# A dilated gated convolution on one core: the steps of every unit in another order

## The chip, the cores and the metric

The kernel runs on one core of one Trainium2 chip. The metric is device time in microseconds; the median of three runs before the change is 309.94 us (309.79 to 312.44).

## The reference, cut to what matters

```python
B, T, D, K = 2, 16000, 144, 15          # x [B,T,D], w [K,D,2D], w_o [D,D], all bfloat16
xp = jnp.pad(x, ((0, 0), (28, 0), (0, 0)))
h = sum(einsum('btc,cd->btd', xp[:, 28 - 2*i : 28 - 2*i + T, :], w[i]) for i in range(K))
z = jnp.tanh(h[..., :D]) * sigmoid(h[..., D:])
return z @ w_o
```

It is a causal convolution with 15 taps two steps apart, 144 channels in and 288 out, then a gate (tanh of one half times sigmoid of the other) and a 144 by 144 projection.

## The kernel before, in words

Time is cut into ten blocks of 3072 steps and one of 1536. A block is two units (units 0 to 19), the last block is unit 20. The convolution is computed in a fast form with fewer products: sums and differences of shifted inputs (tiles `S`, `D`, `E` and the shorter `S2`, `D2`, `E2`, `S4`, `D4`, `E4`, `E42`, and the same of the last 16 channels, `Sr`, `Dr`, `Er`) are multiplied on TensorE (PE) by sums of the weights, and the results are combined on VectorE (DVE).

In each unit the four products `m` = 0 to 3 start in a pair of PSUM banks (`px`, a pool of two pairs, `x_bank`). `V.m` computes a common part there, `Vk.m` copies it on ScalarE (ACT) to the second bank, `Vp.m` adds the private parts. For `m` = 0 and 1, `C` copies the result to single banks (`py`, a pool of three, `y_bank`), `X` and `Y` add further taps in both places, and `tX`, `tY` take them away as `m0`, `m1`. For `m` = 2 and 3, `v.m` takes the pair away as `v2`, `v3`, and `A`, `Ak`, `Ap` compute a second part in another pair or in two single banks. A pair is free for the next user when the instruction that takes it away has run: `tX` or `v` on ACT, or, for a pair that `A` used, `At` on DVE.

On DVE the joining instructions of a unit are `P` (m0 + m1), `s` (m0 - m1, four columns of `y`), `U` (P + v2), `At.2...` (y from U and the second part of product 2), `u3q` (P minus v3, in place) and `At.3...` (y from P and the second part of product 3). `U` reads what `P` wrote, the first `At.2` what `U` wrote, the first `At.3` what `u3q` wrote. All of them are line 205 in the profile, told apart by their tiles: `P<-m,m`, `y<-m,m`, `U<-P,v`, `y<-U,...`, `P<-P,v`, `y<-P,...`.

DVE also derives the input sums: an even unit makes the `E` tiles of its own block, an odd unit the `S`, `D`, `Sr` and `Dr` tiles of the next block. `gt`, `gs` (ACT) and `gm` (DVE) are the gate, which writes `z`. `zT` is a DMA on SP's queue that transposes `z`; `po.g` projects three twelfths of it on PE, `o.g` (ACT) moves the result to `os`, and `ST` stores it. `LD` stands behind `zT`: in an even unit it issues the two transposing loads of `rx` (the last 16 channels of the next block, for both planes e = 0, 1), in an odd unit the loads of `xn`. `Dr` and `Sr` in the next odd unit read `rx`.

The order in which each engine gets its instructions is written out by hand, in four lists of step names (`FIRST` for unit 0, `ODD`, `EVEN`, and `FINAL` for unit 20); a name ending in `.n` is a step of the next unit. Every instruction passes through `K_`, which keeps program order within its engine. The pools give their banks in the order in which the steps ask for them.

Of the kernel before, what the change touches and what calls it, by code (L numbers as in the profile page):

```python
# [15 lines left out]
def kernel(  # L16
# [26 lines left out]
    P = 128  # L43
    B, T, D = x.shape
    K = w.shape[0]
    D2 = w.shape[2]
# [328 lines left out]
    for j in range(8):  # L375
        o = 16 * j
# [187 lines left out]
    U = [dict(id=i, r=r, bi=bi) for i, (bi, r) in enumerate(units)]  # L564
# [238 lines left out]
    def run(ui, names):  # L803
# [1 line left out]
            step(ui, name)  # L805

    FIRST = """
        B wn0.0 wn0.1 wd.1 wd.0 wh.1 wh.0 S D S2 S4 D2 E D4 E2 Sr Dr E4 Er E42 w.0 wt.0 z.15 V.0 w.1 z.3 z.9 z.1 z.5 V.1 Vk.0 wt.1
        w.2 Vk.1 wt.2 Vp.0 w.3 Vp.1 z.12 C.0.1 wt.3 w.8 C.0.0 Y.0.1.main X.0.0.main wn wt.8 w.9 z.10 z.7 wt.9 C.1.0 Y.0.0.main w.4
        X.0.1.main wt.4 X.1.0.main w.5 Y.0.0.rest Y.1.0.main wt.5 tY.0.0 C.1.1 w.6 X.0.0.rest X.0.1.rest Y.1.0.rest X.1.0.rest X.1.1  # L810
        Y.0.1.rest wt.6 tX.0 V.2 tY.1.0 Y.1.1 tX.1 Vk.2 tY.0.1 A.2.1 Vp.2 A.2.0 tY.1.1 Ak.2.1 v.2 Ak.2.0 P U w.7 Ap.2.1.0 V.3 Vk.3
        wt.7 Ap.2.1.1 Ap.2.0.1 At.2.1 Vp.3 Ap.2.0.0 v.3 V.0.n A.3.1 Vk.0.n X.3.0 X.3.1 s At.2.0.0 At.2.0.1 Ak.3.1 Vp.0.n Ap.3.1.0
        Ap.3.1.1 gt.6 C.0.0.n wx u3 tX.3 At.3.1.0 C.0.1.n gs.6 At.3.1.1
    """
    EVEN = """
        B Y.0.0 V.1 Vk.1 tY.0.0 gt.0 X.0.1 X.0.0 Vp.1 po.1 Y.0.1 C.1.0 tX.0 C.1.1 E Y.1.0 X.1.1 V.2 X.1.0 o.1 tY.1.0 gs.0 tY.0.1 Vk.2
        tX.1 Y.1.1 Er E4 E2 gm.6.p A.2.0 Vp.2 po.2 A.2.1 gm.0 E42 zT LD tY.1.1 P Ak.2.0 v.2 Ak.2.1 U A.3.1 Ap.2.0.0 V.3 Ap.2.1.1
        Ap.2.1.0 At.2.0.0 At.2.1 s Vk.3 o.2 Vp.3 v.3 po.3 Ap.2.0.1 A.3.0 V.0.n At.2.0.1 u3q Ak.3.1 o.3 Vk.0.n Ak.3.0 gt.6 ST LL
        Ap.3.1.1 Ap.3.1.0 Vp.0.n Ap.3.0.0 Ap.3.0.1 po.0 At.3.1.0 At.3.1.1 At.3.0 C.0.0.n C.0.1.n gs.6 o.0
    """  # L820
    ODD = """
        B D Y.0.0 X.0.0 X.0.1 V.1 Y.0.1 gt.0 Vk.1 tX.0 tY.0.0 Vp.1 po.1 C.1.0 C.1.1 V.2 Y.1.0 gs.0 Vk.2 o.1 tY.0.1 S Dr X.1.1 X.1.0
        Y.1.1 Vp.2 tY.1.0 tX.1 tY.1.1 v.2 po.2 A.2.1 A.2.0 Ak.2.1 Ak.2.0 o.2 A.3.1 V.3 Ap.2.1.0 Vk.3 Ap.2.1.1 Ap.2.0.0 Vp.3 Ap.2.0.1
        Sr SD4 gm.0 SD2 gm.6.p zT LD P U At.2.1 At.2.0.0 A.3.0 po.3 v.3 Ak.3.0 Ak.3.1 V.0.n Ap.3.0.1 s At.2.0.1 u3q Vk.0.n o.3 gt.6
        ST LL Ap.3.1.0 Ap.3.0.0 Vp.0.n Ap.3.1.1 po.0 At.3.1.0 At.3.0 At.3.1.1 C.0.0.n C.0.1.n gs.6 o.0
    """
    FINAL = """
        B V.1 Y.0.0 X.0.1 Y.0.1 Vk.1 Vp.1 X.0.0 gt.0 tY.0.0 C.1.0 tY.0.1 tX.0 C.1.1 po.1 Y.1.0 gs.0 tY.1.0 E V.2 X.1.0 X.1.1 Y.1.1
        o.1 Vk.2 tX.1 tY.1.1 E4 E2 Er Vp.2 v.2 A.2.1 A.2.0 po.2 Ak.2.0 V.3 Ak.2.1 Vk.3 E42 gm.6.p gm.0 Ap.2.0.0 Ap.2.1.0 Vp.3
        Ap.2.1.1 s.1 P.1 s.0 P.0 gt.4 o.2 v.3 U.1 U.0 At.2.0.0 At.2.1 Ap.2.0.1 po.3 A.3.1 X.3.1 X.3.0 gs.4 o.3 Ak.3.1 At.2.0.1 gt.8  # L830
        gm.4 u3 tX.3 eB gs.8 Ap.3.1.0 At.3.1.0 zT LD q.0 Ap.3.1.1 ev.p0.V At.3.1.1 x6 q.1 eT.A gp.0.2.1 gp.2.1.1 gp.0.2.0 gp.2.1.0
        gp.3.1.0 gp.3.1.1 ev.p1.A gm.8 eT.B mh.0 eT.C ec.A mh.1 ec.B eT.D e3.4 e3.7 ev.p2.V ec.C ev.p3.A ec.D ev.c4.V ev.c7.A e3.10
        e2.0 e2.2 ev.c10.A ev.c2.A ev.c0.A ST sp.0 sp.1 s4 s0
    """
    for ui in range(NU):
        run(ui, FIRST if ui == 0 else FINAL if ui == NU - 1 else (EVEN, ODD)[ui % 2])
# [30 lines left out]
```

## Time and profile before

| what | value |
|---|---|
| median of 3 runs | 309.94 us |
| the profiled execution's own time | 309.88 us |
| its span, first to last instruction | 308.1 us |
| PE, DVE, ACT busy | 296.0, 282.4, 272.8 us |
| matmuls | 2594 |
| granted PE clock | 0.995 |

Busy times count an instruction from its start to its end, and on PE, DVE and ACT the next one starts before the one in front of it has ended; so an engine that is never idle can show fewer busy microseconds than the window has. What an instruction really takes from its queue is the time from its start to the start of the next.

The program has three parts: a start in which weights arrive and are summed (to about 10 us), units 0 to 19 (to about 283 us; two units take 26.6 us), and the last unit with the stores (the last matmul starts at 300.4 us, the last store lands some 6 us later).

### The profile page before, as it was taken

The numbers are of one execution on the slowest core, as the hardware profiler recorded it, in microseconds if no ns is written. First come the engines' busy times: TensorE is split into PE (matmuls) and PEld (weight loads), VectorE is DVE, ScalarE is ACT, GpSimd is POOL, SyncE is SP. The second block draws the span as 40 slices with busy tenths as digits, with TensorE's granted clock in tenths as the row PEclk, the third lists the DMA queues.
The fourth block names the chain that finished last, engine by engine and source line by source line (L and its number), as shares of the span: only waits on it lengthen the run. The fifth ranks groups of instructions, "written<-read, shape, count | busy, mean of one in ns | idle before, by whom it ended". The sixth has DMA issues, their size and how long they took to land.

```text
span 308.1 us, 6789 instructions
## 1 busy us (share of the span) xinstructions
PE 296.0 (96%) x2594; PEld 281.6 (91%) x2594; DVE 282.4 (92%) x399; ACT 272.8 (89%) x614; POOL 32.2 (10%) x69
## 2 busy tenths in 40 slices
PE   8899989999998999999999999999999999999990
PEld 3699989999998999999999999999999999999780
DVE  3999999999999999999999999999999999979790
ACT  4878888989898898989989899899989989898981
POOL 7999100000000000100000000000000000000001
PEclk9999999999999999999999999999999999999997
DMA  8899095858939894993998589596778927644434
GB/s 204 136 81 216 16 171 66 159 106 129 178 62 161 144 169 93 158 200 70 166 157 164 115 120 174 106 161 125 148 130 121 202 47 161 96 93 92 84 80 91
DMA packets 175913, 39.70 MB, mean 129 GB/s; under 512 B 173128, under 2 KB 175688, under 8 KB 175880
## 3 DMA queue, kind: packets, MB, share of 16 engines
q1 hardware_dynamic: 172523, 37.40, 72.1%
q0 software_dynamic: 1824, 1.15, 2.0%
q10 hardware_dynamic: 1533, 0.72, 0.8%
q8 instruction: 20, 0.33, 0.4%
q14 instruction: 13, 0.11, 0.1%
HBM read 3.70 MB, written 11.44 MB: 49 GB/s over the span
## 4 chain that ended last, share of the span: by engine, by line
PE 76%; DVE 8%; DMA 6%; POOL 5%; issue 2%; ACT 1%; POOLq 0%; DVEq 0%
PE px L331 42%; PE py L331 25%; PE po L331 9%; POOL rs L141 3%; DVE SD L205 3%; DMA rx<-rs 2%; DMA zT<-z 2%; DVE y L205 2%; DMA rs<-wz 2%; POOL Wr L309 1%; DVE z L205 1%; DVE P L205 1%; DVE U L205 1%; DMA wo_ab<-in_w_o_dram 0%; DVE Sr L205 0%
## 5 line engine op out<-in xcount | busy, mean ns | idle before, releaser
L331 PEld LDWEIGHTS <-SD 128*128 128x128 bf16 x924 | 114.1, 138 | 2.5 <-issue 0.6
L331 PEld LDWEIGHTS <-E 128*128 128x128 bf16 x737 | 92.7, 143 | 4.6 <-issue 1.6
L572 ACT COPY px<-px 128x288 f32<-128x288 f32 x124 | 49.5, 406 | 7.2 <-PE px L331 5.9
L331 PE MATMUL py<-GN,SD 128*128 128x288 bf16 x336 | 54.5, 286 | 0.2 <-ACT py L572 0.2
L331 PE MATMUL px<-G,SD 128*128 128x288 bf16 x336 | 53.5, 286 | 0.0
L331 PE MATMUL px<-H,SD 128*128 128x288 bf16 x252 | 44.6, 286 | 0.1
L331 PE MATMUL px<-H,E 128*128 128x288 bf16 x252 | 44.6, 286 | 0.0
L331 PE MATMUL po<-wo_ab,zT 128*128 128x144 bf16 x468 | 42.0, 226 | 0.6 <-DMA zT<-z 0.6
L512 ACT CAST os<-po 128x432 bf16<-128x432 f32 x77 | 41.1, 534 | 0.0
L478 ACT ACTIVATE sg<-y 128x864 bf16<-128x864 bf16 (+1 forms) x42 | 39.5, 940 | 0.0
L478 ACT ACTIVATE th<-y 128x864 bf16<-128x864 bf16 (+1 forms) x42 | 39.1, 931 | 0.0
L572 ACT CAST v<-px 128x576 bf16<-128x576 f32 x42 | 27.9, 664 | 12.6 <-PE px L331 12.5
L205 DVE TENSOR_TENSOR E<-E 128x1536 bf16<-128x1536 bf16 (+5 forms) x33 | 38.1, 1178 | 0.0
L331 PEld LDWEIGHTS <-zT 128*128 128x128 bf16 x480 | 35.4, 98 | 2.9 <-DMA zT<-z 0.9
L586 ACT ACTIVATE m<-py 128x288 bf16<-128x288 f32 x84 | 35.7, 445 | 0.0
L572 ACT COPY py<-px 128x288 f32<-128x288 f32 x84 | 31.7, 409 | 1.0 <-DVE y L205 0.5
L205 DVE TENSOR_TENSOR SD<-SD 128x1536 bf16<-128x1536 bf16 (+2 forms) x24 | 30.3, 1271 | 0.0
L586 ACT ACTIVATE m<-px 128x576 bf16<-128x576 f32 x42 | 28.6, 681 | 0.0
L205 DVE TENSOR_TENSOR z<-th,sg 128x864 bf16<-128x864 bf16 (+1 forms) x42 | 24.4, 596 | 3.1 <-ACT sg L478 3.1
L205 DVE TENSOR_TENSOR SD<-xn 128x2048 bf16<-128x2048 bf16 (+1 forms) x22 | 24.8, 1169 | 0.0
L331 PEld LDWEIGHTS <-Er 128*128 128x128 bf16 x168 | 23.9, 142 | 0.2
L331 PE MATMUL px<-Wr,Er 128*128 128x288 bf16 x84 | 24.0, 286 | 0.0
(105 smaller groups left out, 484.6 us busy)
## 6 DMA issues: line engine op xcount, KB each, us to landing
out_dram<-os SPq DMA_DIRECT2D x32, 216.0 KB
rs<-in_x_dram SPq DMA_DIRECT2D x8, 97.0 KB
out_dram<-os SPq DMA_DIRECT2D x4, 168.8 KB
w_all<-in_w_dram ACTq DMA_DIRECT2D x2, 288.0 KB
xnl<-in_x_dram SPq DMA_DIRECT2D x2, 270.0 KB
rxl<-rs SPq DMA_DIRECT2D x2, 256.0 KB
out_dram<-os POOLq DMA_DIRECT2D x2, 216.0 KB, 5.0
xn<-in_x_dram SPq DMA_TRANSPOSE x22
```

The lines of the kernel that those rows point to most:

```text
L141: K_(eng.dma_start(out=bass.AP(o.tensor, o.offset, [[8 * CR, n], [1, 8 * CR]]), in_=wz[0:n, 0:8 * CR]))
L205: return K_(nc.vector.tensor_tensor(out=out_, in0=a, in1=b, op=op))
L309: K_(nc.gpsimd.dma_start(out=Wr[CR * k:CR * (k + 1), 2 + t // 8, :], in_=w[t, CM:D, :]))
L331: K_(nc.tensor.matmul(ps, lhsT=l, rhs=r, start=start and k == 0, stop=stop and k == n - 1, skip_group_check=not start))
L478: K_(nc.scalar.activation(out=cur["g", c0][k][:, 0:n], in_=cur["y"][:, c0:c0 + n, D * k:D * k + D], func=(ACT.Tanh, ACT.Sigmoid)[k]))
L512: K_(nc.scalar.copy(out=dst, in_=po[:, 0:n * D]))
L572: K_(nc.scalar.copy(out=dst, in_=src))
L586: K_(nc.scalar.activation(out=dst, in_=ps, func=ACT.Copy, scale=0.5))
```

## The change

The four lists are replaced; they hold the same steps, and no instruction is added or dropped on PE or DVE. The lists of the units 1 to 19:

```diff
     EVEN = """
-        B Y.0.0 V.1 Vk.1 tY.0.0 gt.0 X.0.1 X.0.0 Vp.1 po.1 Y.0.1 C.1.0 tX.0 C.1.1 E Y.1.0 X.1.1 V.2 X.1.0 o.1 tY.1.0 gs.0 tY.0.1 Vk.2
-        tX.1 Y.1.1 Er E4 E2 gm.6.p A.2.0 Vp.2 po.2 A.2.1 gm.0 E42 zT LD tY.1.1 P Ak.2.0 v.2 Ak.2.1 U A.3.1 Ap.2.0.0 V.3 Ap.2.1.1
-        Ap.2.1.0 At.2.0.0 At.2.1 s Vk.3 o.2 Vp.3 v.3 po.3 Ap.2.0.1 A.3.0 V.0.n At.2.0.1 u3q Ak.3.1 o.3 Vk.0.n Ak.3.0 gt.6 ST LL
-        Ap.3.1.1 Ap.3.1.0 Vp.0.n Ap.3.0.0 Ap.3.0.1 po.0 At.3.1.0 At.3.1.1 At.3.0 C.0.0.n C.0.1.n gs.6 o.0
+        B V.1 Y.0.0 Vk.1 Y.0.1 X.0.1 Vp.1 X.0.0 gt.0 tY.0.0 C.1.0 C.1.1 tX.0 E Er po.1 Y.1.0 X.1.0 V.2 X.1.1 Y.1.1 gm.6.p E2 E4 gs.0
+        tY.0.1 o.1 Vk.2 A.2.0 Vp.2 gm.0 E42 zT LD tX.1 tY.1.0 tY.1.1 Ak.2.0 P v.2 V.3 po.2 Vk.3 Ap.2.0.1 A.3.1 A.2.1 Ap.2.0.0 Ak.2.1
+        o.2 Vp.3 Ap.2.1.1 Ap.2.1.0 v.3 po.3 A.3.0 s U At.2.0.0 At.2.1 At.2.0.1 u3q Ak.3.1 o.3 Ak.3.0 ST LL Ap.3.1.1 V.0.n Ap.3.1.0
+        Vk.0.n gt.6 Ap.3.0.1 Vp.0.n Ap.3.0.0 po.0 At.3.1.1 At.3.1.0 At.3.0 C.0.0.n C.0.1.n o.0 gs.6
     """
     ODD = """
-        B D Y.0.0 X.0.0 X.0.1 V.1 Y.0.1 gt.0 Vk.1 tX.0 tY.0.0 Vp.1 po.1 C.1.0 C.1.1 V.2 Y.1.0 gs.0 Vk.2 o.1 tY.0.1 S Dr X.1.1 X.1.0
-        Y.1.1 Vp.2 tY.1.0 tX.1 tY.1.1 v.2 po.2 A.2.1 A.2.0 Ak.2.1 Ak.2.0 o.2 A.3.1 V.3 Ap.2.1.0 Vk.3 Ap.2.1.1 Ap.2.0.0 Vp.3 Ap.2.0.1
-        Sr SD4 gm.0 SD2 gm.6.p zT LD P U At.2.1 At.2.0.0 A.3.0 po.3 v.3 Ak.3.0 Ak.3.1 V.0.n Ap.3.0.1 s At.2.0.1 u3q Vk.0.n o.3 gt.6
-        ST LL Ap.3.1.0 Ap.3.0.0 Vp.0.n Ap.3.1.1 po.0 At.3.1.0 At.3.0 At.3.1.1 C.0.0.n C.0.1.n gs.6 o.0
+        B D Y.0.0 X.0.1 X.0.0 V.1 Y.0.1 gt.0 Vk.1 Vp.1 tX.0 tY.0.0 C.1.0 C.1.1 Dr S po.1 V.2 Y.1.0 Vk.2 X.1.0 X.1.1 Y.1.1 Vp.2 gs.0
+        tY.1.0 o.1 tY.0.1 tX.1 tY.1.1 v.2 A.2.0 V.3 Vk.3 Ak.2.0 A.3.1 po.2 A.2.1 Ak.2.1 Vp.3 Ap.2.0.0 Ap.2.1.1 Ap.2.1.0 gm.6.p SD4 Sr
+        gm.0 SD2 zT LD P v.3 o.2 A.3.0 Ap.2.0.1 po.3 s U At.2.0.0 At.2.1 Ak.3.0 Ak.3.1 u3q At.2.0.1 o.3 ST LL Ap.3.0.0 V.0.n Vk.0.n
+        gt.6 Ap.3.0.1 Ap.3.1.0 Vp.0.n Ap.3.1.1 po.0 At.3.0 At.3.1.0 At.3.1.1 C.0.0.n C.0.1.n o.0 gs.6
     """
```

`FIRST` and `FINAL` are permuted in the same manner (`FIRST` makes `D` before `S` and asks for `V.1` before `V.0`; `FINAL` puts `s.1` between `P.0` and `P.1`, and the output steps of the last unit in another order).

On DVE this gives, for an even and the following odd unit (the built program's order, by tiles; x2 means two in a row):

```
before  even: E  Er  E4  E2  z  z  E42  P  U  y(U,py)  y(U,px)  y(m,m)  y(U,py)  P'  y(P,py) x2  y(P,px)
        odd:  D  S  Dr  Sr  SD4  z  SD2  z  P  U  y(U,px)  y(U,py)  y(m,m)  y(U,py)  P'  y(P,py)  y(P,px)  y(P,py)
after   even: E  Er  z  E2  E4  z  E42  P  y(m,m)  U  y(U,py)  y(U,px)  y(U,py)  P'  y(P,py) x2  y(P,px)
        odd:  D  Dr  S  z  SD4  Sr  z  SD2  P  y(m,m)  U  y(U,py)  y(U,px)  P'  y(U,py)  y(P,px)  y(P,py) x2
```

Here `P'` is `P<-P,v` (step `u3q`). On the bank pairs the order of users in a unit is V.1, V.2, A.2.1, V.3, A.3.0, V.0.n before, and V.1, V.2, V.3, A.2.1, A.3.0, V.0.n after. The instructions on POOL's and SP's queues keep their order.

More of the change, by code (lines that the diff above doesn't have):

```diff
@@ L807 @@
     FIRST = """
[L808 to L811, printed above, removed]
@@ L812 @@
-        wt.7 Ap.2.1.1 Ap.2.0.1 At.2.1 Vp.3 Ap.2.0.0 v.3 V.0.n A.3.1 Vk.0.n X.3.0 X.3.1 s At.2.0.0 At.2.0.1 Ak.3.1 Vp.0.n Ap.3.1.0
-        Ap.3.1.1 gt.6 C.0.0.n wx u3 tX.3 At.3.1.0 C.0.1.n gs.6 At.3.1.1
+        B wn0.1 wn0.0 wd.1 wd.0 wh.1 wh.0 D S D2 S4 S2 D4 E E2 Sr Dr E4 Er E42 w.0 wt.0 z.9 z.1 z.5 w.1 V.1 wt.1 Vk.1 z.7 z.15 V.0
+        Vk.0 w.2 wt.2 z.10 Vp.1 w.3 z.12 z.3 Vp.0 wt.3 w.8 C.1.0 C.0.1 wt.8 X.1.0.main w.9 Y.0.1.main wt.9 C.0.0 Y.1.0.main w.4
+        Y.0.0.main X.0.1.main wt.4 wn w.5 Y.0.0.rest X.0.0.main wt.5 tY.0.0 C.1.1 X.0.1.rest Y.1.0.rest X.0.0.rest w.6 X.1.0.rest
@@ L814 @@
+        X.1.1 Y.0.1.rest tY.1.0 tX.0 wt.6 V.2 Y.1.1 tX.1 Vk.2 tY.0.1 A.2.1 Vp.2 tY.1.1 Ak.2.1 v.2 P U w.7 A.2.0 Ak.2.0 Ap.2.1.0 V.3
+        Vk.3 wt.7 Ap.2.1.1 Ap.2.0.0 Vp.3 Ap.2.0.1 v.3 A.3.1 wx At.2.1 V.0.n Vk.0.n X.3.0 X.3.1 s At.2.0.0 At.2.0.1 Ak.3.1 Vp.0.n
+        Ap.3.1.0 Ap.3.1.1 gt.6 C.0.0.n u3 tX.3 At.3.1.0 C.0.1.n gs.6 At.3.1.1
     """
     EVEN = """
-        B Y.0.0 V.1 Vk.1 tY.0.0 gt.0 X.0.1 X.0.0 Vp.1 po.1 Y.0.1 C.1.0 tX.0 C.1.1 E Y.1.0 X.1.1 V.2 X.1.0 o.1 tY.1.0 gs.0 tY.0.1 Vk.2
@@ L826 @@
+        tY.1.0 o.1 tY.0.1 tX.1 tY.1.1 v.2 A.2.0 V.3 Vk.3 Ak.2.0 A.3.1 po.2 A.2.1 Ak.2.1 Vp.3 Ap.2.0.0 Ap.2.1.1 Ap.2.1.0 gm.6.p SD4 Sr
+        gm.0 SD2 zT LD P v.3 o.2 A.3.0 Ap.2.0.1 po.3 s U At.2.0.0 At.2.1 Ak.3.0 Ak.3.1 u3q At.2.0.1 o.3 ST LL Ap.3.0.0 V.0.n Vk.0.n
+        gt.6 Ap.3.0.1 Ap.3.1.0 Vp.0.n Ap.3.1.1 po.0 At.3.0 At.3.1.0 At.3.1.1 C.0.0.n C.0.1.n o.0 gs.6
     """
     FINAL = """
-        B V.1 Y.0.0 X.0.1 Y.0.1 Vk.1 Vp.1 X.0.0 gt.0 tY.0.0 C.1.0 tY.0.1 tX.0 C.1.1 po.1 Y.1.0 gs.0 tY.1.0 E V.2 X.1.0 X.1.1 Y.1.1
@@ L829 @@
[L829 to L832, printed above, removed]
@@ L833 @@
-        e2.0 e2.2 ev.c10.A ev.c2.A ev.c0.A ST sp.0 sp.1 s4 s0
+        B Y.0.0 V.1 X.0.0 Y.0.1 Vk.1 Vp.1 tY.0.0 gt.0 C.1.0 tY.0.1 C.1.1 X.0.1 po.1 Y.1.0 tX.0 Y.1.1 Er E E2 gm.6.p E4 gs.0 tY.1.0
+        A.2.0 V.2 X.1.0 X.1.1 tY.1.1 Vk.2 o.1 Ak.2.0 tX.1 Vp.2 v.2 po.2 o.2 gm.0 s.0 E42 Ap.2.0.0 A.2.1 Ak.2.1 P.0 s.1 P.1 U.0
+        At.2.0.0 A.3.1 V.3 Vk.3 gt.4 Ap.2.0.1 Ak.3.1 Ap.2.1.1 Vp.3 Ap.2.1.0 v.3 gs.4 At.2.0.1 U.1 At.2.1 u3 gm.4 po.3 Ap.3.1.0 o.3
+        gt.8 eB gs.8 At.3.1.0 X.3.1 X.3.0 Ap.3.1.1 tX.3 At.3.1.1 gm.8 zT LD q.0 ev.p0.A eT.A x6 ec.A q.1 eT.B gp.0.2.0 gp.0.2.1 mh.0
@@ L834 @@
+        ev.p1.V eT.C gp.2.1.1 gp.3.1.0 gp.3.1.1 gp.2.1.0 mh.1 ec.B e3.4 eT.D e3.7 ec.C ev.p2.A ev.p3.A ev.c4.V ec.D e3.10 e2.0
+        ev.c7.V e2.2 ev.c10.A ev.c0.A ev.c2.A ST sp.0 sp.1 s4 s0
     """
```

## The prediction

> **What bounds the kernel now.** I read the busy times by engine first, then the stretch of one pair of units in the middle, then the queue of DVE, then the waits.
>
> ```profile
> PE 296.0 (96%) x2594; PEld 281.6 (91%) x2594; DVE 282.4 (92%) x399; ACT 272.8 (89%) x614; POOL 32.2 (10%) x69
> 226.98:253.62 26.64, 26.64 (x240) 26.16 (x239) 26.02 (x36) 24.90 (x57) 0.00 (x0) 1.00 0.80 133
> ```
>
> The second line is a table by stretch: length, then busy time and count of PE, weight loads, DVE, ACT, POOL. PE is busy all the time, so its busy time says little; its pitch says more. In the trace two matmuls of 288 columns start 0.122 us apart wherever nothing is waited for, two of 144 columns 0.062 us. A pair of units has 190 of the first and 48 of the second: 190 x 0.1224 + 48 x 0.0622 = 26.2 us, with some 0.1 us of small irregularities 26.3, against 26.63 measured. So PE waits about 0.3 us in a pair. Where, the trace shows:
>
> ```profile
> 240.65 0.29 PE L331 MATMUL py<-Wr,Er 128*128 128x288 bf16 x1
> 240.89 0.28 PE L331 MATMUL px<-NX,E 128*128 128x288 bf16 x1
> ...
> PE px L331 <- DVE y L205: 0.8, 2, 0.6
> ```
>
> The matmul with `NX` (step A.3.0) starts 0.24 instead of 0.12 us behind the one in front. It waits for the pair of banks that A.2.1 used, so for `At.2.1` on DVE. This wait of about 0.11 us stands in every unit, and one of 0.06 us (step Y.1.0, for a copy on ACT) in most odd ones; most are too short to be listed, as matmuls overlap. Together 0.28 us a pair. DVE is what they wait for:
>
> ```profile
> 238.00 0.75 DVE L205 TENSOR_TENSOR P<-m,m 128x1152 bf16<-128x1152 bf16 x1
> 238.85 0.76 DVE L205 TENSOR_TENSOR U<-P,v 128x1152 bf16<-128x1152 bf16 x1
> 239.72 0.45 DVE L205 TENSOR_TENSOR y<-U,py 128x288 bf16<-128x288 bf16 x1
> 240.09 0.74 DVE L205 TENSOR_TENSOR y<-U,px 128x576 bf16<-128x576 bf16 x1
> 240.75 0.75 DVE L205 TENSOR_TENSOR y<-m,m 128x1152 bf16<-128x1152 bf16 x1
> 241.42 0.44 DVE L205 TENSOR_TENSOR y<-U,py 128x288 bf16<-128x288 bf16 x1
> ...
> 244.09 2.35 DVE L205 TENSOR_TENSOR SD<-xn 128x2048 bf16<-128x2048 bf16 x2
> 246.36 0.69 DVE L205 TENSOR_TENSOR Dr<-rx 128x1024 bf16<-128x1024 bf16 x1
> ```
>
> DVE's instructions follow each other without a wait on another engine through the whole pair. Three lines with 1152 elements show what one costs: `y<-m,m` at 240.75 gives way to the next after 0.67 us, `P` at 238.00 after 0.85 and `U` at 238.85 after 0.87, because the next reads what they wrote. A reader right behind its writer costs 0.19 us more. There are six such places in a pair (P to U, U to y, P' to y, in each unit). DVE and PE run in step, DVE a little slower.
>
> **What the change does, part by part.** (1) Pauses. In the new order `y<-m,m` stands between `P` and `U` in both units, and in the odd unit a `y<-U` between `P'` and `y<-P`. Three of six pauses go: 3 x 0.19 = 0.56 us of DVE time a pair. U to y stays in both, P' to y in the even unit.
>
> [...]
>
> (2) Banks. V.3 now comes ahead of A.2.1, so A.3.0 waits for `v.3` on ACT and no longer for DVE. `v.3` takes 0.64 us (`v<-px`) and stands six matmuls and a `po` ahead in the even unit, 6 x 0.12 + 0.37 = 1.1 us, nine matmuls in the odd: covered, with little to spare. What waits for `At.2.1` now is V.0.n. Even unit: `At.2.1` moves back by `y<-m,m` less a pause, 0.67 - 0.19 = 0.48 us; V.0.n stands behind A.3.0 and Ap.3.1.1, 5 x 0.122 = 0.61: the 0.11 wait goes. Odd unit: back by 0.48 + 0.37 (`y<-U,py` now ahead) = 0.85, against four matmuls, 0.49: 0.36 worse, less the 0.37 that DVE gains in the pair up to there, so about the old 0.11 remains. What is queued behind V.0.n is all of PE's next work. I take 0.11 + 0.06 = 0.17 us a pair saved; the ends are 0.1 (Y.1.0 as before) and 0.28 (all waits gone). Nine pairs: -1.5 us, from -0.9 to -2.5. So 0.56 - 0.17 = 0.39 us of slack is left to DVE.
>
> (3) `Dr` ahead of `S`. This is what I think decides. `Dr` needs both transposes of `rx`, which SP issues behind `zT`, which waits for the second `z` of the even unit.
>
> ```profile
> 237.01 1.57 SPq L493 DMA_TRANSPOSE zT<-z  x1
> 238.68 3.86 SPq L202 DMA_TRANSPOSE rx<-rs  x2
> ...
> 32.00 0.69 DVE L205 TENSOR_TENSOR Dr<-rx 128x1024 bf16<-128x1024 bf16 x1 [0.42 <-DMA rx<-rs]
> ...
> 85.70 0.69 DVE L205 TENSOR_TENSOR Dr<-rx 128x1024 bf16<-128x1024 bf16 x1 [0.20 <-DMA rx<-rs]
> ...
> DVE Dr L205 <- DMA rx<-rs: 0.6, 2, 0.4
> ```
>
> Before, `Dr` starts 246.36 - 237.01 = 9.35 us behind `zT`, and still waited twice. The trace's record of DMA landings gives the time from the start of `zT` to the last landing of `rx`, for units 2, 4, ... 16: 9.37, 9.62, 8.76, 8.10, 7.86, 8.43, 8.42, 8.49 us. After, `Dr` comes 1.13 (one `SD<-xn`: half of 244.09 to 246.36) and 0.19 (P to U) earlier: 8.0 us behind `zT` if DVE never waits. Three quarters of the slack, 0.29, lie between the two (the rest falls behind, at the odd unit's last y); and `Dr` starts about 0.05 us after a landing. So a landing later than 8.0 + 0.29 - 0.05 = 8.24 us moves DVE's whole queue, and with it `At.2.1`, V.0.n and PE, by as much. With the old landings: 1.13 + 1.38 + 0.52 + 0 + 0 + 0.19 + 0.18 + 0.25 = 3.65, less 0.4 that the first two cost already (their pairs lasted 26.75 and 26.76 instead of 26.63, and the wait at 85.70 shows as 0.28 more at the next `NX`): +3.3 us. Unit 19 is left out: its block is half as long, and DVE had 1.7 us to wait there. Ends: 0 if all land by 8.24; 8 x 1.38 - 0.4 = +10.6 if all come like unit 4's.
>
> (4) Unit 1. `rx` of block 1 lands at 31.9, set by the start's loads, not by compute. `Dr` starts at 32.00 as before, but `S` and all behind it are 1.13 later. From 32.00, by pitches: Dr 0.60, S 1.13, z 0.52, SD4 1.67, Sr 0.60, z 0.52, SD2 1.05, P 0.67, y 0.67, U 0.86, y 0.37 and `At.2.1` 0.75 to its end: 41.4. V.0.n then, 15 matmuls from its start and a `po` to the end of the unit, 15 x 0.122 + 0.37 = 2.2: unit 2 begins at 43.65, before at 42.59. +1.1 us. Unit 0's new order is behind this landing: D began at 29.22, so it may come up to 1.6 us later for nothing.
>
> (5) `zT` of the odd units. `SD2` now stands behind the second `z`, so `zT` is 1.05 us earlier to its `po.0`. One `po.0`, behind the matmul at 95.78, waited 0.76 us for a landing 5.8 us after `zT`; it would now have 6.1. -0.8 us.
>
> (6) The last unit: same instructions, its PE waits from 283.5 us on add up to 1.3 us. At best these go, and I take as much for the other end: 0, -1.3 to +1.3, as nothing shows which.
>
> Sum against the profiled execution's own 309.88 (span 308.1 and 1.8 around it; the median, 309.94, is the same number): 309.88 - 1.5 + 3.3 + 1.1 - 0.8 + 0 = **312.0 us**, 0.7% slower.
>
> **The rivals.** *The loads come early enough* (the other side): the odd unit's loads and stores now start 1.05 us earlier on SP, so the DMA queues are emptier when `rx` is fetched, and landings drop below 8.24. Then the pair is ruled by PE: 309.88 - 1.5 + 1.1 - 0.8 = 308.7, and if all 0.28 of waits go and the last unit gains too, 306.4. For it: the three landings at 7.9 to 8.1; against it: the early units were worst before any store was under way. It decides at 8.24 + 0.17 = 8.41, where a pair's loss equals its gain, and the median of the eight is 8.43. *Every landing as in units 2 and 4*: 309.88 - 1.5 + 10.6 + 1.1 - 0.8 = 319.3; for it, that a stalled DVE shifts the rest; against it, six of eight. *V.0.n waits more than A.3.0 did*: if the pair orders on ACT or DVE run 0.25 us late in each of 19 units, +4.7 and the 1.5 not saved; landings are then less urgent, 309.88 + 4.7 + 1.1 - 0.8 = 314.9. For it, the thin cover of `v.3`; against it, ACT's 24.9 of 26.6 us. *The pauses stay*, whatever stands between: DVE stays at 26.63 a pair with no slack, `Dr` comes 8.2 behind `zT`, late by 1.2 + 1.5 + 0.6 + 0.3 + 0.3 + 0.3 - 0.4 = 3.8, and 309.88 + 3.8 + 1.1 - 0.8 = 314.0. Against it the 0.67 and 0.85 in the same unit. [...]
>
> **How the numbers follow.** My forecast 0.53, early loads 0.27, all late 0.05, V.0.n 0.12, pauses stay 0.03. One per cent, about what a measurement of this kernel can tell from no change, lies at 306.8 and 313.0. The forecast's own range is 310.3 to 313.7, a fifth of it above 313.0; of early loads three tenths lie below 306.8; of the other three nearly all is above 313.0 (0.2 x 0.53 + 0.2 = 0.31). Faster 0.08, same 0.61, slower 0.31. The range 308.0 to 315.3 leaves out the best of the early loads and the cases with all landings late.
>
> **What would show it.** In the profile after: `U` 0.67 us behind `y<-m,m`, which is 0.67 behind `P`; no gap ahead of `NX`, but one of 0.1 to 1 us ahead of the first `px<-H,SD` behind it in odd units; a wait of `Dr` for `rx` at 32.0 and in most odd units of the first half, several times the 0.6 us of before; unit 2 beginning about 1 us later; quiet pairs of 26.45 us. I am wrong if `Dr` hardly waits beyond unit 1, if the quiet pairs don't shrink, or if PE waits at `NX` for ACT.

## The result, and the profile after

The changed kernel takes 312.19 us (median of 22 runs, 309.79 to 314.54), the kernel before 309.5 us in the same comparison (22 runs, 308.85 to 312.44): a ratio of 1.0082, 95% interval [1.0058, 1.0105]. The ratio is an estimate from the single executions without the slowest of them (314.54), and not the quotient of the two medians. In two later comparisons the ratio was 1.0027 [1.0008, 1.0046] and 1.0025 [1.0012, 1.0038]. So it is a little slower, by 0.3 to 0.8%, and it has become uneven: its runs lie 4.8 us apart in the first comparison, where all but one of the kernel before lie within 1.5 us.

The execution that was profiled is one of the quicker ones: 310.25 us, span 308.5. The busy times by engine, and the stretch of one quiet pair of units (length, then busy time and count of PE, weight loads, DVE, ACT, POOL, then clock, DMA share and GB/s):

```profile
PE 296.2 (96%) x2594; PEld 282.6 (92%) x2594; DVE 282.3 (92%) x399; ACT 275.1 (89%) x614; POOL 31.4 (10%) x69
```

```profile
228.17:254.72 26.55, 26.55 (x240) 26.22 (x239) 26.00 (x36) 25.15 (x56) 0.00 (x0) 1.00 0.79 128
```

The quiet pair is 26.55 us long and was 26.63: 0.08 us shorter. What lies in it shows in DVE's queue (start, duration, tiles, and in brackets the idle time ahead and what ended it):

```profile
238.98 0.76 DVE L205 TENSOR_TENSOR P<-m,m 128x1152 bf16<-128x1152 bf16 x1
239.65 0.76 DVE L205 TENSOR_TENSOR y<-m,m 128x1152 bf16<-128x1152 bf16 x1
240.32 0.76 DVE L205 TENSOR_TENSOR U<-P,v 128x1152 bf16<-128x1152 bf16 x1
241.18 0.45 DVE L205 TENSOR_TENSOR y<-U,py 128x288 bf16<-128x288 bf16 x1
241.83 0.75 DVE L205 TENSOR_TENSOR y<-U,px 128x576 bf16<-128x576 bf16 x1 [0.20 <-PE px L331]
...
245.23 1.22 DVE L205 TENSOR_TENSOR SD<-xn 128x2048 bf16<-128x2048 bf16 x1
246.36 0.69 DVE L205 TENSOR_TENSOR Dr<-rx 128x1024 bf16<-128x1024 bf16 x1
```

`U` starts 0.67 us behind `y<-m,m`, and that 0.67 behind `P`: the pause between them is gone. But DVE now waits 0.20 us for a matmul ahead of `y<-U,px`, where it did not wait before. And `Dr` stands right behind the first `SD<-xn`. In this pair it finds `rx` landed. In the first half of this execution it mostly does not; the same view at the five first such places:

```profile
32.21 0.69 DVE L205 TENSOR_TENSOR Dr<-rx 128x1024 bf16<-128x1024 bf16 x1 [1.20 <-DMA rx<-rs]
...
59.61 0.69 DVE L205 TENSOR_TENSOR Dr<-rx 128x1024 bf16<-128x1024 bf16 x1 [0.65 <-DMA rx<-rs]
...
86.47 0.69 DVE L205 TENSOR_TENSOR Dr<-rx 128x1024 bf16<-128x1024 bf16 x1 [0.26 <-DMA rx<-rs]
...
113.60 0.69 DVE L205 TENSOR_TENSOR Dr<-rx 128x1024 bf16<-128x1024 bf16 x1 [0.50 <-DMA rx<-rs]
...
140.17 0.69 DVE L205 TENSOR_TENSOR Dr<-rx 128x1024 bf16<-128x1024 bf16 x1
```

The waits (total, times, longest) say that PE pays for them:

```profile
PE px L331 <- DVE y L205: 2.7, 4, 1.4
DVE Dr L205 <- DMA rx<-rs: 2.6, 4, 1.2
```

Four waits of DVE for `rx`, 2.6 us, and four waits of PE for DVE, 2.7 us; before they were 0.6 us and 0.8 us. The longest, in PE's queue in unit 1, stands at V.0.n, between the last matmul in front of it and its first:

```profile
40.03 0.28 PE L331 MATMUL px<-Wr,Er 128*128 128x288 bf16 x1
41.70 0.41 PE L331 MATMUL px<-H,SD 128*128 128x288 bf16 x2 [1.39 <-DVE y L205]
```

### The profile page after: what moved, and what is told of

It is laid out like the page before. It is cut to its first block, busy times and chain, and to the rows that moved or that the text cites. A ratio compares the mean times of both kernels' runs of the same rounds, so it can differ in the third digit from the quotient of the medians.

```text
span 308.5 us, 6768 instructions
## 1 busy us (share of the span) xinstructions
PE 296.2 (96%) x2594; PEld 282.6 (92%) x2594; DVE 282.3 (92%) x399; ACT 275.1 (89%) x614; POOL 31.4 (10%) x69
## 4 chain that ended last, share of the span: by engine, by line
## 5 line engine op out<-in xcount | busy, mean ns | idle before, releaser
L572 ACT COPY px<-px 128x288 f32<-128x288 f32 x124 | 50.4, 407 | 11.9 <-PE px L331 10.8
L331 PE MATMUL px<-H,E 128*128 128x288 bf16 x252 | 43.2, 286 | 0.0
L478 ACT ACTIVATE th<-y 128x864 bf16<-128x864 bf16 (+1 forms) x42 | 38.4, 914 | 1.7 <-DVE y L205 1.7
L572 ACT COPY py<-px 128x288 f32<-128x288 f32 x84 | 30.1, 396 | 0.5 <-DVE y L205 0.4
L205 DVE TENSOR_TENSOR z<-th,sg 128x864 bf16<-128x864 bf16 (+1 forms) x42 | 25.1, 597 | 3.2 <-ACT sg L478 3.2
L205 DVE TENSOR_TENSOR SD<-xn 128x2048 bf16<-128x2048 bf16 (+1 forms) x22 | 25.7, 1171 | 0.0
L331 PE MATMUL py<-Wr,Er 128*128 128x288 bf16 x84 | 24.0, 286 | 0.0
```

Source lines behind the costliest of these rows:

```text
L205: return K_(nc.vector.tensor_tensor(out=out_, in0=a, in1=b, op=op))
L331: K_(nc.tensor.matmul(ps, lhsT=l, rhs=r, start=start and k == 0, stop=stop and k == n - 1, skip_group_check=not start))
L478: K_(nc.scalar.activation(out=cur["g", c0][k][:, 0:n], in_=cur["y"][:, c0:c0 + n, D * k:D * k + D], func=(ACT.Tanh, ACT.Sigmoid)[k]))
L572: K_(nc.scalar.copy(out=dst, in_=src))
```

## The experiments

The theory: `Dr` ahead of `S` costs what the landings of `rx` come too late for it, one for one at V.0.n, and everything else in the change is worth a little. Two rivals: the loss sits in the new bank order; or the shorter DVE work itself brings nothing.

### e1: S ahead of Dr

```diff
     ODD =
-        ... C.1.1 Dr S po.1 ...
+        ... C.1.1 S Dr po.1 ...
```

> The changed kernel with one swap: in the odd units S stands ahead of Dr again, as before the change. Theory A (Dr waits for rx, and DVE and PE wait behind it): Dr comes 9.1 us behind zT instead of 8.0, nearly all landings are in time, and unit 1 loses nothing; what is left is the gain, some 0.08 us a pair and 0.8 us at one po.0: about 308.0 us, ratio 0.995, and Dr waits under 0.7 us in all. Theory B (the new order of the bank pairs makes PE wait at V.0.n whatever Dr does): no change from the changed kernel, ratio 1.008, about 312.

Measured: 307.09 us (306.85 to 307.2), ratio 0.9931 [0.9917, 0.9946]. Two names in one list turn a loss into a gain. No wait of `Dr` is left in the trace, and the four runs lie within 0.35 us. DVE's queue in the same stretch:

```profile
241.81 2.35 DVE L205 TENSOR_TENSOR SD<-xn 128x2048 bf16<-128x2048 bf16 x2
244.08 0.68 DVE L205 TENSOR_TENSOR Dr<-rx 128x1024 bf16<-128x1024 bf16 x1
```

Two `SD<-xn` stand ahead of `Dr`, 2.27 us instead of 1.13. The landings did not become earlier: behind `zT` they are 8.23, 9.52, 9.11, 8.03, 8.05, 8.49, 7.64 and 9.24 us, as late as in the changed kernel, so it was the place of `Dr` and not the transfer that had changed. The theory holds; the rival of the bank order falls. It is also the fastest version found, and beats both kernels.

### e3: the kernel before, with Dr ahead of S alone

```diff
     ODD =
-        ... tY.0.1 S Dr X.1.1 ...
+        ... tY.0.1 Dr S X.1.1 ...
```

> The kernel before the change with only this swap: Dr ahead of S in the odd units. Theory A: Dr comes 8.2 us behind zT and DVE has no slack, so late landings cost 3.8 us and unit 1 1.1 us: about 314.4 us, ratio 1.016, and Dr waits 4 to 6 us in all. Theory B: the swap alone is worth nothing, 309.5 us, ratio 1.000.

Measured: 311.84 us (311.07 to 313.29), ratio 1.0092 [1.0062, 1.0121]. The swap alone, in the old order, costs 2.6 us. The sign is A's, the size is about half of it. In its waits:

```profile
DVE Dr L205 <- DMA rx<-rs: 4.3, 6, 1.3
```

Six waits, of which the profile lists one of 1.31 and others of 0.26 to 1.02. The profiled execution took 313.29 us, the longest of the four: 4.1 us above the kernel before, with 4.3 us of these waits.

### e8 and e11: the changed kernel itself, beside others

> The changed kernel itself once more, for a second profile: its executions lie between 309.8 and 314.5 us where those of e1 lie within 0.4 us. Theory A: the spread is that of the landings of rx, which e1 hides. Then in this profile, whatever its time, the excess over e1 (307.1) is what PE waits at V.0.n, one for one: the sum of these waits beyond the usual 0.07 us is the time less 307.1, to within 0.7 us. Rival: the excess is spread over the units, in the granted clock or in other waits.

> The changed kernel itself, for the comparison of e10_unit1_S_before_Dr on the same chip. Between 309.9 and 312.2 us by the chips so far (ratio 1.003 to 1.008), with 2 to 4 us of waits for rx in odd units.

Measured: 309.85 us (308.77 to 311.48), ratio 1.0027 [1.0008, 1.0046], and 310.08 us (309.53 to 311.27), 1.0025 [1.0012, 1.0038]. With the first profile there are three of the changed kernel, and the prediction's threshold can be tried unit by unit. It said that a landing later than 8.24 us behind the start of `zT` moves PE by the excess. The table has the late landings (from the trace's record of landings), the excess over 8.24, and how much longer than its usual 0.07 us PE waited at the next V.0.n (from starts of matmuls, less the 0.122 us of a matmul). In the other units up to 16 there is no excess, and the extra wait is at most 0.02.

| profile | landing of `rx`, us behind `zT` (unit) | excess | PE's extra wait |
|---|---|---|---|
| first | 9.00 (2), 8.68 (4), 8.86 (6) | 0.76, 0.44, 0.62 | 0.69, 0.33, 0.62 |
| e8 | 8.43 (2), 8.92 (4), 9.23 (6), 8.67 (12), 9.16 (16) | 0.19, 0.68, 0.99, 0.43, 0.92 | 0.17, 0.58, 0.97, 0.40, 0.88 |
| e11 | 8.86 (2), 8.66 (4), 9.28 (6), 8.37 (8), 8.67 (12), 9.16 (16) | 0.62, 0.42, 1.04, 0.13, 0.43, 0.92 | 0.57, 0.33, 1.03, 0.10, 0.39, 0.89 |

Fourteen landings, and the waits follow within 0.11 us; so do the five late ones of e10 below. With unit 1 (0.19 us in e8) the extra waits of e8 add up to 3.2 us, and its execution of 310.0 us is 3.15 above that of e1 (306.85). But e1 has 0.3 us of such waits too, 0.18 of them in unit 1. So 2.9 us of the difference are this wait; 0.3 more arise behind the last matmul, and 0.1 is gained at the start. In the first profile the waits are 2.8 of 3.4 us above e1 (unit 1 also starts 0.55 later), in e11 3.5 of 3.9. In these three executions the difference between the two orders is nearly all this wait.

### e2: rx fetched earlier

```diff
     EVEN =
-        B V.1 Y.0.0 ...          # LD behind zT issues both transposes of rx
+        B LR V.1 Y.0.0 ...       # LR issues them here, ahead of zT
```

> The changed kernel with Dr still ahead of S, but SP issues the two loads of rx at the start of each even unit, some 6.5 us earlier and ahead of zT, not behind it. Theory A: no wait of Dr but in unit 1, where the start's loads set the landing (1.2 us); about 309.1 us, ratio 0.999. Theory B: 312, ratio 1.008. Theory C (what costs is the order D, Dr, S itself, as V.0.n needs S later): 312 too, with PE waiting at V.0.n and no wait at Dr.

Measured: 315.21 us (312.94 to 316.14), ratio 1.0184 [1.0142, 1.0227]: slower than any theory said. `Dr` never waits any more, so what A said of the landings is right, and no wait at V.0.n exceeds its usual one by more than 0.02 us behind unit 1, so C falls; the price came from elsewhere. PE now waits four times for `zT`, 5.5 us as the waits list it, where the kernel before waited once; and SP's queue waits for the gather. The waits in this kernel, of PE and then of SP's queue:

```profile
PEld L331 <- DMA zT<-z: 6.5, 4, 2.6
PE po L331 <- DMA zT<-z: 5.5, 4, 2.4
```

```profile
SPq L202 <- DMA rs<-in_x_dram: 17.5, 8, 4.7
```

and SP's queue where the longest wait of PE arose, with that wait in PE's queue:

```profile
125.21 2.27 SPq L134 DMA_DIRECT2D rs<-in_x_dram  x2
131.19 2.96 SPq L202 DMA_TRANSPOSE rx<-rs  x2
134.26 1.74 SPq L493 DMA_TRANSPOSE zT<-z  x1
...
139.38 0.55 PE L331 MATMUL po<-wo_ab,zT 128*128 128x144 bf16 x6 [2.37 <-DMA zT<-z]
```

The transposes of `rx` read what the gather `rs<-in_x_dram` wrote, and wait for it at the head of SP's queue (17.5 us in all, eight times). Here they go out at 131.19; `zT`, whose `z` was done at 130.42, goes out at 134.26 behind them and lands at 139.33, and the `po.0` that needs it waits 2.4 us. Measured against the kernel before, the four units behind such a wait start 0.80, 1.30, 2.27 and 1.57 us later than the unit in front of each does: 5.9 us, and the span of 311.1 less 5.9 is 305.2, e1's 305.0. One wait was taken away and a larger one put in its place, by what stands behind the moved issue in its queue.

### e10: S ahead of Dr in unit 1 alone

```diff
-        run(ui, ... (EVEN, ODD)[ui % 2])
+        run(ui, ... ODD.replace("Dr S", "S Dr") if ui == 1 else (EVEN, ODD)[ui % 2])
```

> The changed kernel with S ahead of Dr in unit 1 alone; all other odd units keep Dr ahead of S. Theory A (unit 1 has a share of its own in the waits for rx, as the prediction's +1.1 us has it): 0.7 to 1.1 us below the changed kernel on the same chip, and the first TensorE wait at V.0.n gone, with the waits of units 3 and later left. Theory B (the waits follow one another: what unit 1 saves is waited for again in unit 3, since rx of unit 2 then lands as late against an earlier Dr): within 0.3 us of the changed kernel, with a longer wait in unit 3.

Measured: 309.32 us (308.31 to 310.4), ratio 1.0005 [0.999, 1.0019], beside 310.08 of the changed kernel, so 0.8 us less by the medians, but the two intervals touch. In the two profiles V.0.n of unit 1 waits 0.25 instead of 0.57 us, only 0.3 less (e1 has the 0.25 too); the wait in unit 3 is the same (0.68 and 0.64), so B's longer one there does not show. The size of unit 1's share is not settled by this run.

### e4: the kernel before, with the pauses taken out and the old bank order

```diff
     EVEN =
-        ... tY.1.1 P Ak.2.0 ... At.2.1 s Vk.3 ...
+        ... tY.1.1 P s Ak.2.0 ... At.2.1 Vk.3 ...
     ODD =
-        ... LD P U ... Ap.3.0.1 s At.2.0.1 ...
+        ... LD P s U ... Ap.3.0.1 At.2.0.1 ...
```

> The kernel before the change with only s moved between P and U in odd and even units, the banks as before. Theory A: two pauses of 0.19 us a pair go, but At.2.1 comes 0.48 us later in each unit and A.3.0 still waits for its bank pair; PE waits some 0.3 us more in each of 19 units, about 315 us, ratio 1.018 (at least 1.005). Rival (the pauses are what counts): PE's 0.28 us of waits a pair go, 307 us, ratio 0.992.

Measured: 315.96 us (315.28 to 316.21), ratio 1.0222 [1.0205, 1.0239], as the first theory had it. Each pair takes 27.35 instead of 26.63. The waits:

```profile
DVE y L205 <- PE py L331: 8.4, 19, 0.5
PE px L331 <- DVE y L205: 5.6, 16, 0.8
```

With `s` ahead of `U`, `At.2.1` comes later; PE waits for it at A.3.0 (16 times), and DVE then waits for what PE makes next (19 times). So the new place of `s` is a loss in the old bank order. The next experiment keeps the new bank order and puts `s` back.

### e6: e1 with all pauses put back

```diff
     EVEN =
-        ... A.3.0 s U At.2.0.0 At.2.1 At.2.0.1 ...
+        ... A.3.0 U At.2.0.0 At.2.1 s At.2.0.1 ...
     ODD =
-        ... po.3 s U At.2.0.0 At.2.1 Ak.3.0 Ak.3.1 u3q At.2.0.1 ...
+        ... po.3 U At.2.0.0 At.2.1 s Ak.3.0 Ak.3.1 At.2.0.1 u3q ...
```

> As e1 (S ahead of Dr, new bank order), but U directly behind P again and s behind At.2.1, u3q directly ahead of At.3: the three pauses of 0.19 us a pair are back, At.2.1 comes 0.48 us earlier. If the freed pauses make the quiet pair 26.55 instead of 26.63, the pair goes back to 26.63 or a little less: 307.1 + 9 x 0.08 = 307.8, ratio 0.9955, and DVE has no slack. If the bank order alone did it (PE no longer behind At.2.1), 307.0 or less, ratio 0.993.

Measured: 315.05 us (314.35 to 315.46), ratio 1.0187 [1.0169, 1.0205]. Both expectations were wrong, by 7 and 8 us. A pair takes 27.39 us, 0.84 more than e1's. DVE's queue at the place where e1 and the changed kernel wait 0.20 us:

```profile
244.32 0.45 DVE L205 TENSOR_TENSOR y<-U,py 128x288 bf16<-128x288 bf16 x1
245.46 0.76 DVE L205 TENSOR_TENSOR y<-U,px 128x576 bf16<-128x576 bf16 x1 [0.68 <-PE px L331]
246.13 0.75 DVE L205 TENSOR_TENSOR y<-m,m 128x1152 bf16<-128x1152 bf16 x1
```

`y<-m,m` (0.67 us) is missing ahead of it and one pause is back, so DVE arrives 0.48 us earlier and waits 0.68 instead of 0.20 for the matmuls of A.2.1; `y<-m,m` must still be done behind. 0.48 of waiting and three pauses of 0.19 make 1.05 us more, of which 0.84 came through. So the step between `P` and `U` does two things: it covers the pause, and it fills a time in which DVE has nothing to join yet. The second, 0.48 us, is worth nearly as much as the three pauses together, 0.57. With e4 this shows that the two halves of the change need each other: either one without the other is 6 to 7 us longer than the kernel before.

### e9: e1 with one pause put back

```diff
     ODD =
-        ... Ak.3.1 u3q At.2.0.1 o.3 ...
+        ... Ak.3.1 At.2.0.1 u3q o.3 ...
```

> The order of e1_S_before_Dr, but in odd units with At.2.0.1 directly behind the step that it depends on and u3q behind it, instead of u3q between: one dependency pause of 0.19 us more in every pair, and At.2.0.1 about 0.67 us earlier on VectorE. Theory A (VectorE sets the length of a quiet pair, so that every pause counts in full): 9 pairs x 0.19 = +1.7 us on the 307.1 of e1_S_before_Dr, 308.8 us, ratio 0.997. Theory B (VectorE still waits for TensorE a little in each pair, 0.39 us by the order's slack, and the pause goes into that wait): no change, 307.1 us, ratio 0.993.

Measured: 308.03 us (307.51 to 308.99), ratio 0.9964 [0.9947, 0.9981], between the two theories. A quiet pair takes 26.61 us against 26.55 in e1: of the 0.19 us, some 0.07 come through (9 x 0.07 = 0.6 us) and 0.12 go into a wait. Which one, the distance of DVE's starts tells: the two `y<-P,py` at the end of the odd unit took 0.85 us in e1 and take 0.73 here. The other 0.3 us between the medians (308.03 and 307.09) are not explained by this; in the one trace, of an execution of 308.92 us, `rx` of block 1 lands at 32.38, `Dr` waits 0.40 us for it, and unit 1 is 0.54 us longer than in e1. So late start loads can cost in e1's order too.

### e7 and e5: the second z ahead of SD2, and the two ends

```diff
     e7: ODD
-        ... gm.0 SD2 zT LD P ...
+        ... SD2 gm.0 zT LD P ...
     e5: FIRST and FINAL as in the kernel before
```

> As e1, but SD2 ahead of the second z in the odd units, as before the change, so zT of the odd units comes 1.05 us later. Where a landing of zT takes over 5 us po.0 waits again: the profile before shows this once, 0.76 us; about 0.8 us more than e1, 307.9, ratio 0.9955. Rival: that wait was a chance, 307.1.

> The changed kernel with S ahead of Dr (as in e1_S_before_Dr, 307.1 us, 0.9931), and with FIRST and FINAL as before the change; so only the lists of units 1 to 19 are new. From the traces: the last matmul to the end took 7.7 us before and 7.1 with the new FINAL, and unit 20's matmuls 16.9 and 16.8. If the new ends are worth that, this run loses 0.6 to 0.8 us against e1: 307.8, ratio 0.9955. If FIRST or FINAL hide a loss as the prediction's bounds (up to 1.3 us) allow, it gains: 306.

Measured: e7 307.86 us (307.63 to 308.22), ratio 0.9956 [0.9942, 0.997]; e5 307.78 us (307.52 to 311.22), ratio 0.9963 [0.9939, 0.9986]; both as expected. Their intervals touch e1's, so what follows rests on the traces. In e7, PE's queue has the wait of the kernel before again, at the same `po.0`:

```profile
95.67 0.55 PE L331 MATMUL po<-wo_ab,zT 128*128 128x144 bf16 x6 [0.48 <-DMA zT<-z]
```

In e5 the time from the last matmul's start to the end is 7.54 us; it was 7.67 in the kernel before and is 7.07 in e1, 7.09 in the first profile of the changed kernel, but 7.39 in e8 and 7.37 in e11. From the start of unit 20 to the end it is 24.5 and 24.6 us with the old list and 23.9 to 24.3 with the new one. So the new lists at the ends are worth 0.3 to 0.7 us, most of it behind the last matmul.

## Why the prediction was right, and where its terms were off

The forecast was 312.0 us in a range of 308.0 to 315.3; measured were 312.19. The deciding step, (3), is the one that the runs confirm best. That 312.0 met 312.19 to 0.2 us is luck: terms were off in opposite directions, the profiled execution took 310.25, and the medians of the two later comparisons were 309.85 and 310.08. The range holds them all, but the two later medians are nearer to the other side, 308.7, than to the forecast; it is the waits that decide for (3), and not the times.

- **(1) Pauses.** Right: 0.67 and 0.67 in place of 0.85 and 0.87. In the Trainium skill, "VectorE: DVE Perf Modes", section "The DRAIN you can't avoid", has the next instruction wait for the pipeline to empty, but lets one that isn't held start earlier; the section behind it, "Two Vector instructions with no wait between them", has a held one start only when every earlier one has finished. The trace agrees with that exception for an instruction that doesn't read what the one in front wrote: 0.67 us from start to start at a duration of 0.76. The rival that the pauses stay is refuted by the same rows.
- **(2) Banks.** The mechanism right, the size off by a factor of two: 0.08 us a pair were saved, not 0.17, so 9 pairs gave 0.7 and not 1.5 us. The two waits at A.3.0, 0.11 each, did go, and none came at `NX`. V.0.n in the odd unit waits 0.07. The 0.06 at Y.1.0, which was counted as gained, stayed. And one wait of 0.06 was not foreseen: in the even unit the weight load of the first matmul of Ap.2.0.1 waits for `E42`, and the second matmul starts 0.06 late behind it (by the starts of the matmuls). 0.22 - 0.07 - 0.06 = 0.09, the 0.08 within rounding.
- **The slack of DVE.** The 0.39 us left over are there, as waits of DVE for PE: 0.20 ahead of `y<-U,px`, and by DVE's starts 0.11 at the two `y<-P,py` of the odd unit (0.85 for 0.74) and 0.07 at those of the even one (0.84 for 0.77), together 0.38. But it isn't one store of slack that any extra pause may draw on. In e9 0.12 of 0.19 found cover, in e6 0.2 of 1.05.
- **(3) `Dr` ahead of `S`.** Right in mechanism, place and threshold: the table of fourteen landings. Predicted were 3.65 us in the units behind unit 1 (with the landings of the kernel before); the profiles show 1.6, 3.0 and 3.3. The price is that of the landings in each execution. The 0.4 us taken off for the two late landings of before is right by the waits at `NX` (0.11 and 0.28 more than usual); the two pair lengths beside it are not: by PE's starts these pairs took 26.78 and, less the 0.76 at `po.0`, 26.92.
- **(4) Unit 1.** It was put at +1.1 us, from a landing at 31.9. In the first profile the landing came at 32.11 and unit 2 began 0.73 us later against unit 1's start than before; in e8 it came at 30.08, and unit 2 began 0.54 us earlier, as in e1. So the term was one draw of the start's loads, and 0.54 us that unit 1 gains in the new order were missing. In the first profile unit 1 itself also started 0.58 us later than before, for which the sum has no term; in e8 it started 0.1 earlier. e10 did not settle the rest.
- **(5) `zT` of the odd units.** Right: -0.8 forecast; the wait of 0.76 us is gone in the changed kernel and e1, and 0.65 of it (by the matmuls' starts) are back in e7.
- **(6) The ends.** Put at 0; -0.7 us measured in the first profile and -0.4 in e8 and e11, inside its bounds.
- **The early loads**, the other side at 308.7 us, did not happen: the landings stayed at 7.6 to 9.3 us behind `zT`. Its counterargument, that the early units were worst before any store was under way, holds for unit 2 at most: in the profile before, stores go out at 55.87 and 70.28 us, ahead of unit 4's fetch at 77.70. e1 shows the time without the wait, 307.1, and why it is below 308.7: unit 1 gains 0.5 there instead of losing 1.1, and the ends gain 0.7, while the pairs gain 0.8 less than forecast; together 307.2.
- **V.0.n waits more, pauses stay, all late**: none of the three. The executions measured reach from 309.79 to 314.54 us, and the prices of the first two, 314.9 and 314.0, lie at or near their upper end, so the time alone could not have told them apart; the waits did.

The sum by what was measured gives the profiled executions. The first: 309.88 - 0.7 (pairs) - 0.4 (waits of before that the new ones contain) + 1.6 (late landings) + 0.7 (unit 1) + 0.6 (its start) - 0.8 (`zT`) - 0.7 (ends) = 310.2, measured 310.25. e8: 309.88 - 0.7 - 0.4 + 3.0 - 0.5 - 0.1 - 0.8 - 0.4 = 310.0, measured 310.0. e11: 309.88 - 0.7 - 0.4 + 3.3 - 0.2 + 0.2 - 0.8 - 0.4 = 310.9, measured 310.77.

What made the median of the first comparison 2 us longer than its own profile stays open, as no trace of such a longer execution was taken. Later landings are one candidate, argued from the three traces and not shown. The granted clock (the share of TensorE's full speed that was let through, as a mean over the execution) is another: the eight of the 22 executions with less than 0.992 took 312.25 to 314.54 us, the fourteen others 309.79 to 313.75. In e5, with `S` ahead of `Dr`, one of ten executions took 311.22 us at 0.987, and the nine others 307.52 to 308.16 at 0.992 to 0.996. In the kernel before no such link shows: in e5's comparison its 20 executions had 0.991 to 0.996 and took 308.8 to 310.06. Whether the clock made those executions longer or only went down with what did, no run tells.

## What to carry to other kernels

When a step that reads a transfer is moved ahead, compare the time of its start with every recorded landing and not with the mean: each late landing counted in full here, and the early ones gave nothing back. Before an issue is moved on a queue, look at what it waits for there and what stands behind it; e2 took away 3 us of waits and paid 6. And freed time on one of two engines in step is worth only what the waits between the two allow: 0.56 us a pair became 0.08.

## What was not expected of the hardware

The two transposes of `rx`, the same in every block, land 7.6 to 9.6 us behind the start of `zT`, and part of this repeats from execution to execution: for unit 6 it was 8.86, 9.23 and 9.28 us in the three profiles of the changed kernel, 9.11 in e1; for unit 8 it was 8.04, 7.94, 8.37 and 8.03. Unit 16 had 8.01 in the first profile, and 9.16, 9.16 and 9.24 in e8, e11 and e1. What sets it stays open.
